# All of an expert's turned output tiles in one group after the second product, and the overflow scatter made dependent on the scatters before it

## The chip, the cores and the metric

The kernel runs on one core of a Trainium2 chip. TensorE (PE in the profile; PEld is its weight load) multiplies and transposes into PSUM, VectorE (DVE) and ScalarE (ACT) read PSUM and compute, GpSimd (POOL) issues the gathers and scatters, and SyncE (SP) issues the other transfers. The engines run side by side, each through its own list of instructions in order, and wait for each other on semaphores. The metric is the device time of one execution in microseconds (us); lower is better.

## The reference

A thresholded attention feeds a mixture of experts in which a hash of the token's id chooses the expert.

```python
# attention, per head: keep scores within tau of the row's maximum
scores = scale * np.matmul(q, k.transpose(0, 1, 3, 2))
thresh = np.max(scores, axis=-1, keepdims=True) - tau
scores = np.where(scores >= thresh, scores, -1e9)
attn = softmax(scores);  attn_out = np.matmul(attn, v)          # (8, 8, 576, 64)
x = attn_out.transpose(0, 2, 1, 3).reshape(4608, 512)
# experts: every token goes to one of 8
expert_idx = token_ids * np.int64(2654435761) % np.int64(8)
for e in range(8):
    mask = expert_idx == e
    out[mask] = np.maximum(x[mask] @ w1[e], 0) @ w2[e]          # 512 -> 1024 -> 512
```

With these inputs the experts get 598, 596, 571, 565, 599, 533, 570 and 576 tokens.

## The kernel before

The first 525 us are the attention, which the change does not touch. Then follow the experts, one after the other, some 59 us each. An expert has room for 600 tokens (CAP, as 19 blocks of 32 less 8). Tokens beyond the 600th would be taken by a loop at the end of the program (`For_i`, L1038), which runs once for each tile of 128 overflow tokens; its trip count is loaded from `ov_i` (L1037). No expert here has more than 599 tokens, so the loop's body is not entered; but the instructions that load the count, compare it, branch and wait stand in the program on every engine.

Layer 1 and layer 2 of an expert are each computed by `seven`: a matrix product done as seven block products with sums on DVE before and after. `layer1` calls it twice (g = 0 and 1), `layer2` once. A block product takes one PSUM tile from `bank2()`; the pool `ps_m` has four of these[...]. A fifth `bank2()` has to wait until an earlier tile has been read. In this text the products of one `seven` are numbered 1 to 7 in their order: 1 gives p1 (copied by ACT), 2 gives c11, 3 gives u2, 4 gives u3, 5 gives c21, 6 gives u4 and c22, 7 gives c12. All but the first are read by an addition on DVE (L794). A hook, `side(g, step)`, is called after the products: step 0 after product 2, step 1 after 3, step 2 after 4, step 3 after 5.

Layer 2 leaves its result feature-major in `oT`. `put_out` brings it into token order: for each tile of up to 128 tokens, eight TensorE transposes into a `bank2()` (L923; two tiles of tokens share a bank2), one ACT copy into `o_sb` (L934), and one indirect scatter of the rows to `out` from POOL's queue (L938, in `put_rows`). The five tiles of expert e-1 are put out during layer 1 of expert e, g = 0: tiles 0 and 1 at step 0, tiles 2 and 3 at step 1, tile 4 at step 2. So one group of transposes stands between products 2 and 3, one between 3 and 4, one between 4 and 5. The pool `m_o` has three `o_sb` buffers: the copy of tile 3 waits until the scatter of tile 0 has landed, and that of tile 4 until the scatter of tile 1 has.

For the last expert tile 0 is put out within layer 2, tiles 1 to 3 in `middle`, within `last_tile`, and `last_tile` computes the remaining 120 tokens with plain products (L908), copies them with ACT into `o_end` (L912) and scatters those rows. The scatters of `put_rows` are declared to have no dependence on each other (`declare_no_dep`), since every token has one slot; the scatter inside the overflow loop belongs to the same group.

The order of each engine's instructions is written out by hand (`manual_schedule`), while the framework places the waits, picks the PSUM tile that a `bank2()` gets, and splits the program into blocks around the loop. In the built program the scatter of `o_end` stands on POOL's list behind the loop, after a block in which each engine waits for every transfer and every other engine.

Of the kernel before, what the change touches and what calls it, by code (L numbers as in the profile page):

```python
# [9 lines left out]
FP32 = mybir.dt.float32  # L10
# [10 lines left out]
def kernel(  # L21
# [12 lines left out]
    nc = tc.nc  # L34

    B, H, D, S = qT.shape
    N, DIN = out.shape
    E, _, F = w1.shape
    P = 128
    HP = H // 2  # L40
    NP = B * HP
    CO = DIN // P
# [14 lines left out]
    KT, NB = 5, 19  # L57
# [4 lines left out]
    FIRST = [P * k for k in range(KT)]  # L62
    TROWS = [P] * (KT - 1) + [CAP - FIRST[-1]]
# [19 lines left out]
    ident = consts.tile([P, P], FP32, name="ident")  # L83
# [16 lines left out]
    gidx = consts.tile([P, E, KT], I32, name="gidx")  # L100
# [30 lines left out]
    with tc.tile_pool(name="a_q", bufs=1) as a_q, \  # L131
# [25 lines left out]
        oT = a_o.tile([P, 64 + S], FP32, name="oT")  # L157
        av = ps_av.tile([P, 2, 512], FP32, name="av")
        kts, rss, recs, scs, nss, stats, ws = {}, {}, {}, {}, {}, {}, {}
# [112 lines left out]
        def turn_w(n, j):  # L272
            tr = ps_tr.tile([P, 2, 512], FP32, name="tr")
            if n % NS == 0:
                cols = [(64 + P * c, P * c) for c in range(NC)]
            else:
                cols = [(P * c, P * c) for c in (range(4), range(4, 9))[j]]
            turn(tr, w_bufs[n % NW], cols)
            return tr
# [354 lines left out]
        with tc.manual_schedule():  # L634
            make_identity(nc, ident[:])

            tr = ps_tr.tile([P, 2, 512], FP32, name="tr")
# [18 lines left out]
            for n in range(LAST + NS + 1):  # L656
                p, s = divmod(n, NS)
# [22 lines left out]
                q = p - 1  # L680
# [10 lines left out]
                if n == LAST:  # L691
                    for k in (0, 2):
                        tr = ps_sc.tile([P, 2, 512], FP32, name="sc")
# [11 lines left out]
                if turned:  # L705
                    tr = turn_w(m, 0)
# [6 lines left out]
                if n == LAST:  # L713
                    tr = ps_sc.tile([P, 2, 512], FP32, name="sc")
# [12 lines left out]
                if s in (3, 4) and turned:  # L727
                    tr = turn_w(m, 1)
# [11 lines left out]
                if s in (0, 1) and turned:  # L740
                    tr = turn_w(m, 1)
# [12 lines left out]
            for h in range(4):  # L754
                rows, n = slice(32 * h, 32 * h + 32), (NB - h + 3) // 4
# [3 lines left out]
            for g in range(4):  # L759
                rows, n = slice(32 * g, 32 * g + 32), min(KT, NB - KT * g)  # L760
# [6 lines left out]
            tr = ps_tr.tile([P, 2, 512], FP32, name="tr")  # L767
            early_xT(tr, 0, KT, CO - 1, CO)

    with tc.tile_pool(name="m_x", bufs=1) as m_x, \  # L770
# [3 lines left out]
        F2, C2, FH, D2, NG = F // 2, CO // 2, FO // 2, DIN // 2, FO // 4  # L774
        xT_bufs = [xT_0, m_x.tile([P, CO, CAP], FP32, name="xT_1")]
        xq = m_x.tile([P, DIN // 32, 32 * KT], FP32, name="xq")
        oT = m_x.tile([P, CO, CAP], FP32, name="oT")
# [7 lines left out]
        CHL = 32 * (NB - 4) // 2  # L785

        def bank2():
            return ps_m[0].tile([P, 2, 512], FP32, name="bank2")
# [40 lines left out]
        def sums_w2(e):  # L829
            s1 = None  # L830
            if e == E - 1:
                spare = w_pool.tile([P, CO, F], FP32, name="w1_sb")
                s1 = w_tiles["s1"] = spare[:, :, 0:D2]
            return left(*w2_blocks(w_tiles[e, 2]), triple(w2_s, 0, FH), s1)
# [4 lines left out]
        def sums_h(e, c0, c1):  # L839
            return right(*h_blocks(c0, c1, half2(e)), triple(h_s, c0, c1, half2(e)))  # L840
# [71 lines left out]
                nc.scalar.copy(o_sb[0:rows, c0:c1], ps[0:rows, 0, 0:c1 - c0])  # L912
            put_rows(o_sb[0:rows], idx[0:rows])

        def put_out(e, kts):

            tr = bank2()
            for i, kt in enumerate(kts):
                rows = TROWS[kt] if e < E - 1 or kt < KT - 2 else 2 * CHL - FIRST[kt]
                for co in range(CO):  # L920
                    for r in range(2):
                        half, c0 = slice(64 * r, 64 * r + 64), D2 * i + 64 * co
                        nc.tensor.transpose(tr[0:rows, r, c0:c0 + 64],  # L923
                                            oT[half, co, FIRST[kt]:FIRST[kt] + rows],
                                            ident[half, half])
            for i, kt in enumerate(kts):
                rows = TROWS[kt] if e < E - 1 or kt < KT - 2 else 2 * CHL - FIRST[kt]
                o_sb = m_o.tile([P, DIN], FP32, name="o_sb")
                dst = o_sb[0:rows].rearrange("p (c r q) -> p r c q", c=CO, r=2)
                src = tr[0:rows, :, D2 * i:D2 * i + D2].rearrange("p r (c q) -> p r c q", c=CO)  # L930
                if e == E - 1 and kt % 2:
                    nc.vector.tensor_copy(dst, src)
                else:
                    nc.scalar.copy(dst, src)  # L934
                put_rows(o_sb[0:rows], gidx[0:rows, e, kt:kt + 1])

        def put_rows(o_sb, idx):
            inst = nc.gpsimd.indirect_dma_start(  # L938
                out=out[:, :], out_offset=bass.IndirectOffsetOnAxis(ap=idx, axis=0),
                in_=o_sb, in_offset=None, bounds_check=N - 1, oob_is_err=False)  # L940
            inst = getattr(inst, "ins", inst)
            tc.declare_no_dep(inst, group="rows", reason="every token has one slot: distinct rows")
            tc.add_to_no_dep_group("rows", inst)

# [34 lines left out]
        with tc.manual_schedule():  # L979
            for e in range(E):  # L980
                more = e + 1 < E
                turns = turn_x(e + 1) if more else []

                if e > 0:
                    w2_work, h_work = sums_w2(e), sums_h(e, 0, 2)

                    def side1(g, step):
                        if g == 0:
                            run(w2_work)
                            if step == 0:  # L990
                                put_out(e - 1, (0, 1))
                            elif step == 1:
                                put_out(e - 1, (2, 3))
                            elif step == 2:
                                put_out(e - 1, (4,))
                        else:
                            run(h_work)
                        if step > 2:
                            run(turns, 1 if g == 0 else 2)

                    layer1(e, side1)
                    run(sums_h(e, 2, FH), 4)
                if e + 2 < E:
                    load_w1(e + 2)
                x_work = (sums_w1(e + 1) + sums_x(e + 1)) if more else []

                def side2(step):
                    if step == 0:
                        run(turns, len(turns))
                        if e + 2 < E:  # L1010
                            fetch(e + 2)
                    else:
                        run(x_work, 2)
                    if not more and step == 4:
                        put_out(e, (0,))

                layer2(e, side2)
                run(x_work, len(x_work))
                if e + 2 < E:
                    load_w2(e + 2)  # L1020


            def middle():
                put_out(E - 1, (1, 2))
                put_out(E - 1, (3,))

            last_tile(middle)

# [9 lines left out]
        with tc.For_i(0, n_ov, 1) as it:  # L1038
            ex = nc.values_load(ov_i[0:1, bass.ds(it, 1)], engines=[mybir.EngineType.Pool],
                                min_val=0, max_val=E - 1)  # L1040
            w1_sb = w_pool.tile([P, CO, F], FP32, name="w1_sb")
            w2_sb = w_pool.tile([P, FO, DIN], FP32, name="w2_sb")
            nc.gpsimd.dma_start(
                out=w1_sb[:],
                in_=w1[bass.ds(ex, 1)].rearrange("o (c p) f -> p (o c) f", p=P))
            nc.gpsimd.dma_start(
                out=w2_sb[:],
                in_=w2[bass.ds(ex, 1)].rearrange("o (c p) d -> p (o c) d", p=P))
            idx = m_x.tile([P, 1], I32, name="idx_ov")
            idx_odd = m_x.tile([P, 1], I32, name="idx_odd")  # L1050
            for table, dst in zip(slot_dram, (idx, idx_odd)):
                nc.gpsimd.dma_start(out=dst[:], in_=table[bass.ds(it * P + E * SL, P), :])
            nc.vector.tensor_tensor(out=idx[:], in0=idx[:], in1=idx_odd[:], op=ALU.min)
            gather(x_dram, xg_bufs[0][:], idx[:, 0:1])
            tr = bank2()
            for co in range(CO):
                nc.tensor.transpose(tr[:, 0, co * P:co * P + P], xg_bufs[0][:, co * P:co * P + P],
                                    ident[:])
            nc.vector.tensor_copy(xT_0[:, :, 0:P], tr[:, 0].rearrange("p (c q) -> p c q", c=CO))
            relu_layer(w1_sb, xT_0)  # L1060
            o_ps = bank2()
            for fo in range(FO):
                nc.tensor.matmul(o_ps[:, 0], lhsT=h_0[:, fo, 0:P], rhs=w2_sb[:, fo],
                                 start=(fo == 0), stop=(fo == FO - 1))
            o_sb = m_o.tile([P, DIN], FP32, name="o_sb")
            nc.scalar.copy(o_sb[:], o_ps[:, 0])
            put_rows(o_sb[:], idx[:, 0:1])


# [32 lines left out]
```

## Time and profile before

| | |
|---|---|
| median of 3 runs | 950.64 us (949.88 to 950.99) |
| the profiled execution | 951.87 us, of which the profile's span is 950.2 us |
| PE busy over the span | 935.2 us (98%) |
| DVE, ACT, POOL busy | 733.9, 478.6, 306.2 us |
| output transposes, L923 | 312 recorded, in 23 groups |
| copies of turned tiles, L934 and L932 | 37 and 2 |
| scatters of rows, L938 | 39 from `o_sb`, 1 from `o_end` |
| TensorE clock granted, mean | 0.996 |

A row of a timeline gives the start in us from the span's start, the busy time, the engine, the line, the operation with "output <- input", and the count of merged instructions; in square brackets stands the idle time of the engine before it and what ended it. The times of matmuls are starts that were recorded and ends that are modelled, so distances between starts are used here.

### The profile page before, as it was taken

Reading aid. Unit: us, or ns where it says so; the run is one execution under the profiler, and the core shown is the slowest. Engines: PE = TensorE matmul, PEld = TensorE weight load, DVE = VectorE, ACT = ScalarE, POOL = GpSimd, SP = SyncE. Lnnn points to the kernel's source line nnn. Section 1 sums busy time; section 2 is a strip of 40 time slices with the busy share of each in tenths; the row PEclk is TensorE's granted clock in tenths of the full one; section 3 lists DMA queues with packets and bytes.
Section 4 is the critical chain, followed back from the end, with each engine's and each line's share of the span. In section 5 each row is a group of like instructions: output and inputs, shape, how many; then the busy total and the mean of one; then the engine's idle time right before and its main releaser. Section 6 shows DMA issues by size and latency. Waiting matters only on the chain. (4 is left out here: it accounts for less than half of the span.)

```text
span 950.2 us, 21041 instructions
## 1 busy us (share of the span) xinstructions
PE 935.2 (98%) x7779; PEld 645.2 (68%) x7779; DVE 733.9 (77%) x1638; ACT 478.6 (50%) x778; POOL 306.2 (32%) x413
## 2 busy tenths in 40 slices
PE   7999999999999999999999999999999999999996
PEld 4666666666666666666667777777777777777784
DVE  7999999999999999999456756756667566575541
ACT  6988888888898898888320211202112031120310
POOL 4233233237766733565043300403013030110202
PEclk9999999999999999999999999999999999999999
DMA  7355456445438857841017444344443445311101
GB/s 177 87 142 131 107 134 148 100 124 137 105 90 212 210 158 156 196 103 35 26 37 216 156 93 174 96 147 160 115 151 91 143 157 142 128 55 32 50 1 51
DMA packets 113510, 113.31 MB, mean 119 GB/s; under 512 B 31182, under 2 KB 88014, under 8 KB 113408
## 3 DMA queue, kind: packets, MB, share of 16 engines
q1 hardware_dynamic: 105168, 92.84, 36.9%
q0 software_dynamic: 7808, 18.91, 6.7%
q8 instruction: 63, 1.03, 0.5%
q14 instruction: 39, 0.32, 0.1%
q10 hardware_dynamic: 432, 0.21, 0.1%
HBM read 81.99 MB, written 21.72 MB: 109 GB/s over the span
## 5 line engine op out<-in xcount | busy, mean ns | idle before, releaser
L247 ACT ACTIVATE w<-ns,nmx 128x576 f32<-128x576 f32 x288 | 220.3, 776 | 32.8 <-DVE ns L233 32.5
L258 DVE SCALAR_TENSOR_TENSOR w<-ns,thr,w 128x576 f32<-128x576 f32 x288 | 225.9, 816 | 0.7 <-POOL thr L240 0.6
L233 DVE TENSOR_SCALAR_CACHE_REDUCE ns<-sc 128x576 f32<-128x576 f32 x288 | 205.3, 744 | 4.4 <-PE sc L222 3.5
L222 PE MATMUL sc<-k_sb,q 64*128 64x288 f32 (+1 forms) x1280 | 178.7, 423 | 1.1 <-DVE drop L650 0.6
L269 PEld LDWEIGHTS tr<-ident,w 64*128 64x128 f32 x2624 | 106.6, 139 | 88.4 <-ACT wT_b L290 26.4
L240 POOL TENSOR_SCALAR thr<-nmx,drop 128x2 f32<-128x2 f32 (+1 forms) x160 | 103.4, 646 | 184.0 <-DVE ns L233 173.3
L938 POOL DMA_INDIRECT out_dram<-o_sb,gidx x39 | 47.7, 1222 | 292.3 <-ACT o_sb L934 278.9
L269 PE MATMUL tr<-ident,w 64*128 64x64 f32 x2624 | 139.0, 230 | 2.6 <-ACT wT_a L290 2.0
L869 ACT COPY p<-bank 128x600 f32<-128x600 f32 (+1 forms) x22 | 14.4, 654 | 201.4 <-PE bank L859 200.6
L222 PEld LDWEIGHTS sc<-k_sb,q 64*128 64x128 f32 (+1 forms) x1280 | 92.5, 178 | 23.1 <-DVE ns L233 9.9
L300 PE MATMUL av<-wT_a,v 128*64 128x320 f32 (+1 forms) x704 | 100.7, 419 | 0.0
L859 PE MATMUL bank<-h,w_sb 128*128 128x300 f32 (+1 forms) x384 | 97.3, 410 | 0.9 <-DVE h L609 0.9
L866 ACT ACTIVATE h<-h 128x600 f32<-128x600 f32 x56 | 39.4, 703 | 114.6 <-DVE h L794 114.1
L290 ACT COPY wT_a<-tr 128x512 f32<-128x512 f32 (+1 forms) x128 | 81.7, 638 | 19.8 <-PE tr L269 19.5
L859 PE MATMUL bank<-xT,w_sb 128*128 128x300 f32 x336 | 89.4, 416 | 0.0
L859 PEld LDWEIGHTS bank<-h,w_sb 128*128 128x128 f32 x384 | 72.9, 190 | 22.9 <-DVE h L609 1.3
L290 ACT COPY wT_b<-tr 128x512 f32<-128x512 f32 (+1 forms) x128 | 81.2, 635 | 6.6 <-PE tr L269 4.3
L300 PE MATMUL av<-wT_b,v 128*64 128x256 f32 x640 | 83.2, 389 | 0.0
L859 PEld LDWEIGHTS bank<-xT,w_sb 128*128 128x128 f32 x336 | 63.9, 190 | 21.0
L859 PE MATMUL bank<-h_s,w_s 128*128 128x300 f32 (+1 forms) x256 | 64.3, 410 | 0.0
L300 PEld LDWEIGHTS av<-wT_a,v 128*64 128x64 f32 x704 | 43.9, 137 | 28.8 <-issue 0.3
L859 PE MATMUL bank<-x_s,w_s 128*128 128x300 f32 x224 | 61.5, 423 | 0.0
(147 smaller groups left out, 1110.3 us busy)
## 6 DMA issues: line engine op xcount, KB each, us to landing
w_sb<-in_moe_w_dram SPq DMA_DIRECT2D x16, 2048.0 KB
q<-in_q_dram SPq DMA_DIRECT2D x62, 288.0 KB
v<-in_v_dram SPq DMA_DIRECT2D x32, 256.0 KB
x_scratch<-xm SPq DMA_DIRECT2D x32, 256.0 KB
xT<-xq SPq DMA_DIRECT2D x84, 80.0 KB
k_sb<-in_k_dram SPq DMA_DIRECT2D x31, 144.0 KB
k_sb<-in_k_dram SPq DMA_DIRECT2D x32, 112.0 KB
x_scratch<-xg SPq DMA_DIRECT2D x9, 256.0 KB
```

What stands on the lines that cost most here:

```text
L222: nc.tensor.matmul(sc[out_rows, i, 0:S2], lhsT=q_sb[rows, h, q0:q1], rhs=k_sb[rows, h], start=True, stop=True)
L233: nc.vector.tensor_scalar(out=ns[:].rearrange("p (i s) -> p i s", i=2), in0=sc[:, :, 0:S2], scalar1=-1.0, scalar2=None, op0=ALU.mult, op1= ...
L240: nc.gpsimd.tensor_scalar(out=thr[:, 0:j + 1], in0=stats[n][0][:, 0:j + 1], scalar1=drop[:], scalar2=None, op0=ALU.add)
L247: nc.scalar.activation(w, nss[n, j][:], AF.Exp, bias=stats[n][0][:, j:j + 1], scale=-1.0)
L258: nc.vector.scalar_tensor_tensor(out=w, in0=nss.pop((n, j))[:], scalar=stats[n][1][:, j:j + 1], in1=w, op0=ALU.is_le, op1=ALU.mult, accum_ ...
L269: nc.tensor.transpose(dst[:, r, 64 * c:64 * c + 64], src[rows, c0:c0 + P], ident[rows, rows])
L290: nc.scalar.copy(dst, tr[:, :, 0:64 * n_c].rearrange("p r (c q) -> p r c q", c=n_c))
L300: nc.tensor.matmul(av[64 * j:64 * j + 64, g, c0:c1], lhsT=v_sb[:, c, 64 * j:64 * j + 64], rhs=wT[g][:, i, c0:c1], start=(c == 0), stop=stop)
L859: nc.tensor.matmul(ps[:, i, 0:width], lhsT=x[:, c, c0:c0 + P], rhs=y[:, c], start=c == 0, stop=c == n_k - 1)
L866: nc.scalar.activation(c, c, AF.Relu)
L869: nc.scalar.copy(p1, product(a11, b11))
L938: inst = nc.gpsimd.indirect_dma_start(out=out[:, :], out_offset=bass.IndirectOffsetOnAxis(ap=idx, axis=0), in_=o_sb, in_offset=None, bound ...
```

## The change

`put_out` takes several groups of tiles. It first takes a `bank2()` for each group, then issues the transposes of all groups, and then the copies and scatters. During layer 1 it is called once, at step 0, with the groups (0, 1), (2, 3) and (4,); the calls at steps 1 and 2 are gone. In `middle` one call with (1, 2) and (3,) takes the place of two. `put_rows` gets a flag `ordered`; the overflow loop passes True, and its scatter is then left out of the group of scatters without dependences.

```diff
-        def put_out(e, kts):
-
-            tr = bank2()
-            for i, kt in enumerate(kts):
-                rows = TROWS[kt] if e < E - 1 or kt < KT - 2 else 2 * CHL - FIRST[kt]
-                for co in range(CO):
-                    for r in range(2):
-                        half, c0 = slice(64 * r, 64 * r + 64), D2 * i + 64 * co
-                        nc.tensor.transpose(tr[0:rows, r, c0:c0 + 64],
-                                            oT[half, co, FIRST[kt]:FIRST[kt] + rows],
-                                            ident[half, half])
-            for i, kt in enumerate(kts):
-                rows = TROWS[kt] if e < E - 1 or kt < KT - 2 else 2 * CHL - FIRST[kt]
-                o_sb = m_o.tile([P, DIN], FP32, name="o_sb")
...
+        def put_out(e, *groups):
+
+            def rows_of(kt):
+                return TROWS[kt] if e < E - 1 or kt < KT - 2 else 2 * CHL - FIRST[kt]
+
+            trs = [bank2() for _ in groups]
+            for tr, kts in zip(trs, groups):
+                for i, kt in enumerate(kts):
+                    rows = rows_of(kt)
+                    for co in range(CO):
+                        for r in range(2):
+                            half, c0 = slice(64 * r, 64 * r + 64), D2 * i + 64 * co
+                            nc.tensor.transpose(tr[0:rows, r, c0:c0 + 64],
+                                                oT[half, co, FIRST[kt]:FIRST[kt] + rows],
+                                                ident[half, half])
+            for tr, kts in zip(trs, groups):
+                for i, kt in enumerate(kts):
+                    rows = rows_of(kt)
+                    o_sb = m_o.tile([P, DIN], FP32, name="o_sb")
+                    dst = o_sb[0:rows].rearrange("p (c r q) -> p r c q", c=CO, r=2)
+                    src = tr[0:rows, :, D2 * i:D2 * i + D2].rearrange("p r (c q) -> p r c q", c=CO)
+                    if e == E - 1 and kt % 2:
+                        nc.vector.tensor_copy(dst, src)
+                    else:
+                        nc.scalar.copy(dst, src)
+                    put_rows(o_sb[0:rows], gidx[0:rows, e, kt:kt + 1])
+
-        def put_rows(o_sb, idx):
+        def put_rows(o_sb, idx, ordered=False):
             inst = nc.gpsimd.indirect_dma_start(
                 out=out[:, :], out_offset=bass.IndirectOffsetOnAxis(ap=idx, axis=0),
                 in_=o_sb, in_offset=None, bounds_check=N - 1, oob_is_err=False)
             inst = getattr(inst, "ins", inst)
+            if ordered:
+                return
             tc.declare_no_dep(inst, group="rows", reason="every token has one slot: distinct rows")
             tc.add_to_no_dep_group("rows", inst)
...
                             if step == 0:
-                                put_out(e - 1, (0, 1))
-                            elif step == 1:
-                                put_out(e - 1, (2, 3))
-                            elif step == 2:
-                                put_out(e - 1, (4,))
+                                put_out(e - 1, (0, 1), (2, 3), (4,))
...
             def middle():
-                put_out(E - 1, (1, 2))
-                put_out(E - 1, (3,))
+                put_out(E - 1, (1, 2), (3,))
...
             nc.scalar.copy(o_sb[:], o_ps[:, 0])
-            put_rows(o_sb[:], idx[:, 0:1])
+            put_rows(o_sb[:], idx[:, 0:1], True)
```

In the built program the order changes in two places. On PE the 40 transposes of an expert stand together between products 2 and 3. On POOL the scatter of `o_end` stands ahead of the loop's instructions instead of behind them. The orders on ACT and DVE stay as they were.

More of the change, by code (lines that the diff above doesn't have):

```diff
@@ L913, in last_tile @@
             put_rows(o_sb[0:rows], idx[0:rows])
-        def put_out(e, kts):
-            tr = bank2()
-            for i, kt in enumerate(kts):
-                rows = TROWS[kt] if e < E - 1 or kt < KT - 2 else 2 * CHL - FIRST[kt]
-                for co in range(CO):
-                    for r in range(2):
-                        half, c0 = slice(64 * r, 64 * r + 64), D2 * i + 64 * co
-                        nc.tensor.transpose(tr[0:rows, r, c0:c0 + 64],
-                                            oT[half, co, FIRST[kt]:FIRST[kt] + rows],
-                                            ident[half, half])
-            for i, kt in enumerate(kts):
-                rows = TROWS[kt] if e < E - 1 or kt < KT - 2 else 2 * CHL - FIRST[kt]
-                o_sb = m_o.tile([P, DIN], FP32, name="o_sb")
[L929 to L935, printed above, removed]
```

## The prediction

> **What bounds the kernel now.** I read the page's first part, then the timeline of one expert boundary, the waits of the expert stage, and the end.
>
> ```profile
> PE 935.2 (98%) x7779; PEld 645.2 (68%) x7779; DVE 733.9 (77%) x1638; ACT 478.6 (50%) x778; POOL 306.2 (32%) x413
> ```
>
> TensorE never rests for long; in the expert stage a window of 24.40 us (761.9 to 786.3) has DVE busy 15.26, ACT 7.55 and POOL 9.32 us. What shortens TensorE's chain there shortens the kernel, unless a product then waits for its PSUM tile. The timeline at the fifth of the seven groups (layer 1 of e = 5), with the rows that the change touches:
>
> ```profile
> 766.13 0.72 PE L923 MATMUL bank<-ident,oT 64*128 64x64 f32 x16
> 766.30 0.78 DVE L794 TENSOR_TENSOR h<-bank,p 128x600 f32<-128x600 f32 x1 [3.33 <-PE bank L859]
> ...
> 766.77 2.29 PE L859 MATMUL bank<-x_s,w_s 128*128 128x300 f32 x8
> 767.00 1.22 DVE L791 TENSOR_TENSOR w_s<-w_sb 128x1024 f32<-128x1024 f32 x1
> ...
> 767.73 1.05 ACT L934 COPY o_sb<-bank 128x512 f32<-128x512 f32 x2
> 768.57 1.03 POOL L938 DMA_INDIRECT out_dram<-o_sb,gidx  x1 [34.03 <-ACT o_sb L934]
> ...
> 768.99 0.71 PE L923 MATMUL bank<-ident,oT 64*128 64x64 f32 x16
> ...
> 769.63 2.29 PE L859 MATMUL bank<-x_s,w_s 128*128 128x300 f32 x8
> ...
> 769.80 1.22 DVE L794 TENSOR_TENSOR w_sb<-w_sb 128x1024 f32<-128x1024 f32 x1
> 769.90 1.99 POOL L938 DMA_INDIRECT out_dram<-o_sb,gidx  x1 [0.30 <-issue]
> 771.43 0.58 ACT L934 COPY o_sb<-bank 128x512 f32<-128x512 f32 x1 [1.10 <-DMA out_dram<-o_sb,gidx]
> ...
> 771.85 0.43 PE L923 MATMUL bank<-ident,oT 64*88 64x64 f32 x8
> ...
> 772.21 2.29 PE L859 MATMUL bank<-x_s,w_sb 128*128 128x300 f32 x8
> ...
> 774.33 2.18 PE L859 MATMUL bank<-xT,w_sb 128*128 128x300 f32 x8
> ```
>
> Two things are to be seen. Products with transposes on both sides start 2.22 us before what follows them (766.77 to 768.99), the one with transposes ahead of it only 2.12 (772.21 to 774.33); the next starts 2.02 later, at 776.35. And ACT's fourth copy (771.43) did not wait for TensorE but for the landing of a scatter, because there are three `o_sb`. The end, from the timeline:
>
> ```profile
> 940.36 0.95 POOL L938 DMA_INDIRECT out_dram<-o_sb,gidx  x1 [0.30 <-issue]
> 941.55 0.27 ACT L912 COPY o_end<-bank 120x128 f32<-120x128 f32 x1 [1.27 <-PE bank L908]
> 944.94 1.02 POOL L938 DMA_INDIRECT out_dram<-o_end,gidx  x1 [3.63 <-issue]
> ```
>
> and, from the answer for the program's last line, the drains (shortest, median, longest in ns):
>
> ```profile
> L1098 POOLq DRAIN  x3: 46/109/4632, 944.7 to 949.9; - x3
> ```
>
> The last rows were ready at 941.82, but their scatter began at 944.94: it stands behind the loop's wait for all transfers, which ended with the landing of the scatter of 940.36, at 943.11. The closing drain on POOL took until 949.33.
>
> **The change part by part.** Time t is counted from an expert's first transpose (766.13 above).
>
> *Transposes on TensorE.* Before: 0.64 (16 transposes) + 2.22 + 0.64 + 2.22 + 0.36 (8) + 2.12, so product 6 starts at t = 8.20 (774.33). After: 40 transposes, then 2.12 + 2.02 + 2.02. Eight more transposes cost 0.64 - 0.36 = 0.28, so 40 cost 0.36 + 4 x 0.28 = 1.48; the 24 in one run in the last tile took 0.87 (936.06 to 936.93), which by the same steps gives 1.38. I take 1.42, and product 6 could start at t = 7.58: 0.62 less, 4.3 us for seven experts. If nothing waits.
>
> *The waits that come in their place.* Three groups now hold PSUM tiles at once, so the products behind them need these back sooner. The waits in the built program: product 3 waits for DVE's c11 (ends t = 0.95 by 766.30 + 0.78 less 766.13; needed at 1.42), product 4 for ACT's second copy (2.65; needed at 3.54). In the first group (e = 1) product 5 waits for u2, which DVE can finish at 1.42 + 2.32 + 0.78 = 4.5 (needed 5.56), and product 6 for the fourth copy. In the other six groups *product 5* waits for the fourth copy. That copy hangs on scatter 0, whose time the change leaves: c11's Relu, two copies, scatter at t = 2.45, landing 2.72 to 2.78 us later in five groups, 3.25 in the first and 3.24 in the last. The copy ended at t = 5.82 to 5.89 in five groups, 6.39 in the first, 6.34 in the last. Product 5 could start at 5.56. TensorE goes on 0.06 after an ACT copy (in the attention a copy ended at 300.35, the load began at 300.40). Five groups: product 5 at 5.90, product 6 at 5.90 + 2.12 = 8.02 instead of 8.20, saving 0.18 each. Last group: 6.40 + 2.12 = 8.52, losing 0.32. First group: its tile is asked for at 7.58, after 6.39, so the full 0.62. Sum: -0.62 - 5 x 0.18 + 0.32 = **-1.2 us**, of 4.3. Ends: -4.3 if no product waited, and +1.3 if all six landed at 3.25 (-0.62 + 6 x 0.32).
>
> Behind these waits: the tail products (6, 7 and g = 1) move with product 5. Product 7 needs the fifth copy, which ended at t = 8.2 at the latest and is wanted at 10.0. DVE's additions follow the products and have slack (15.26 of 24.40 us).
>
> *A rule that could spoil the fourth copy.* The Trainium skill (SBUF — State Buffer, "Who interferes with whom") says that a VectorE instruction with two SBUF inputs and a GpSimd instruction that reads SBUF exclude each other, and the one that started first holds the port to its end. The row shows it: scatter 1 (769.90) took 1.99 instead of 1.03, with DVE's `w_sb` sum (769.80 to 771.02) across its start. If such a sum fell across scatter 0, the fourth copy would come 1.0 later and six groups would lose 6 us. By the trace it doesn't: the `w_s` sum (t = 0.87 to 2.09) stays where it is, ahead of scatter 0 (2.45), and the `w_sb` sum moves later with u2, to about 4.4, after the start of scatter 1 (3.8). So I count nothing; scatter 1 may even get 1.0 shorter, which helps the fifth copy alone.
>
> *`middle`.* Its 24 transposes already stood together, orders and banks' readers stay: 0.
>
> *The scatter of `o_end`.* It no longer stands behind the loop's waits. It can start 0.28 after ACT's copy (768.57 less the first copy's end at 768.29), so at 942.10 instead of 944.94, and is issued by 943.12. POOL's own loading and testing of the count (about 1 us) now comes behind it, but beside its flight. It lands 2.7 to 3.3 later (2.70 and 2.74 for the two before it; 3.27 for itself): about 945.0. Then the block of waits: the slowest engine, DVE, left it 1.53 after the last landing before (943.11 to 944.63), so 946.5. POOL is at its drain by then. The drain is the unknown: it took 4.63 with the scatter ahead of it unfinished, 0.11 and 0.05 the other two times. Nothing is in flight now, so I take 0.1, the row it is like; the upper end is 4.63 again. From the drain's end to the span's end: 950.17 - 949.33 = 0.85. Sum: 946.5 + 0.05 + 0.85 = 947.4, **-2.75 us**. With a landing at 3.3: -2.4; with a second full drain (946.0 + 4.63 + 0.85 = 951.4): +1.3.
>
> *The ordered flag.* The loop's body isn't entered (the profile has no row of its lines), so its new waits cost 0; the flag's trace in this run is only the new place of the `o_end` scatter.
>
> Sum in the profiled execution: 951.87 - 1.2 - 2.75 = 947.9. The median of runs is 1.2 lower, 950.64, and both savings are distances that don't depend on that, so 950.64 - 3.95 = 946.7; a little of the landing spread taken in, **946.8 us**.
>
> **The rivals.** (a) Full gain: the fourth copy isn't waited for, because scatter 0 lands sooner or TensorE hides it; -4.3 - 2.7, 943.6. Against it, five groups agree on the landing within 0.06. (b) Late landings: scatters 0 and 1 now fly closer together (before, scatter 1 was held back by 1 us), and if all six groups show 3.25, the stage gives +1.3 and the sum is 949.2. Against: the scatters of 937.79 and 939.08 were also close, and landed in 2.68 and 2.70. (c) The end doesn't do what it should: the drain costs its 4.63 wherever it starts; +1.3 - 1.2, 950.7.
> (d) Slower: the clock. The Trainium skill (TensorE: Matmul & The Clock Gate, Part 4 and Part 1) says that transposes don't count as activity for the clock gate, and an idle window of 3.4 us halves the clock. By that rule a longer run of transposes could drop the clock in each of seven groups, each time for a window that does 1.7 us less work: +11.9 - 3.95, 958.6. The row of the window that holds the last group says otherwise (stretch, its length, busy us of PE, PEld, DVE, ACT, POOL, then the granted clock, DMA share, GB/s):
>
> ```profile
> 931.00:941.50 10.50, 10.50 (x69) 7.59 (x67) 1.94 (x3) 1.06 (x2) 3.92 (x4) 1.00 0.19 73
> ```
>
> It has the run of 24 transposes, and the clock is 1.00. 40 take 1.4 us, still well under such a window, with products around them. It decides only if the clock in the boundary falls below 1.00; a drop in two or three groups would eat the gain.
>
> **How the numbers follow.** My forecast, the end as worked out and part of the stage's gain, 945.6 to 948.7: 0.68. (a) 0.08; (b) and other small losses in the stage, 948.7 to 950: 0.12; (c) 0.07; (d) or a like stall 0.05. The range that leaves out (d), (c) and half of (a): 944.6 to 949.4. A measurement of this kernel can tell about 0.2%, 1.9 us, so faster means under 948.74: 0.68 + 0.08 + 0.03 = 0.79; slower, (d) and a little of (c): 0.06; same 0.15.
>
> **What would show it.** In the changed profile: one run of 40 transposes per expert, with the product behind it 1.4 us later; in six of seven groups a wait of TensorE for ACT's `o_sb` before product 5, some 0.3 us, 0.8 where the landing is late, and none in the first; a distance from first transpose to product 6 of 8.0 instead of 8.20; the scatter of `o_end` at about 0.3 after its copy; a closing drain of 0.1. I am wrong if the fourth copy moves, if the drain stays at 4.6, or if the granted clock falls.

## The result, and the profile after

The changed kernel took 948.48 us (median of 10 runs, 947.81 to 950.67) beside 951.04 us for the kernel before on the same chip (10 runs, 949.88 to 952.02). The ratio is 0.9976, with a 95% interval of 0.9967 to 0.9986: about 2.3 us less, between 1.3 and 3.1. The forecast was 946.8 us with a range of 944.6 to 949.4. The direction and the range held; the gain is smaller than the 3.8 us of the forecast (950.64, its median of before, less 946.8).

The profiled execution of the changed kernel took 950.67 us, the longest of its ten, with a span of 948.96 us; the one of before took 951.87, with 950.17. I split both spans at three marks that both traces have: the first output transpose (of e = 1), the last one (in the last tile), and the end of ACT's copy into `o_end`.

| stretch, us | before | after | difference | forecast |
|---|---|---|---|---|
| start to first output transpose (attention, first expert) | 530.93 | 531.70 | +0.77 | 0 |
| first to last output transpose ("the stage") | 405.86 | 404.38 | -1.48 | -1.2 |
| last transpose to the end of the `o_end` copy | 5.04 | 5.04 | 0 | 0 |
| end of the `o_end` copy to the end of the span ("the end") | 8.35 | 7.85 | -0.50 | -2.75 |
| span | 950.17 | 948.96 | -1.21 | -3.95 |

The first row is not the change's work: ahead of the first output transpose the program is the same, and in the other kernels below, with the same attention, this mark lies anywhere from 528.92 to 537.55 us. The two stretches that the change touches give -1.98 us together, inside the interval of the timed runs. So the stage did a little more than foretold, and the end did a fifth of it. Each stretch is read from one profile of each kernel; how well such readings repeat is told under "Each part alone".

Busy time hardly moved, as the page's first part shows (935.2 us of PE before):

```profile
PE 933.1 (98%) x7779; PEld 645.1 (68%) x7779; DVE 734.1 (77%) x1638; ACT 478.1 (50%) x778; POOL 306.1 (32%) x413
```

The timeline of the changed kernel at the fifth of the seven groups (start, busy us, engine, line, operation, count; in brackets the idle time before it and what ended it):

```profile
765.70 1.44 PE L927 MATMUL bank<-ident,oT 64*128 64x64 f32 x40
...
767.07 4.31 PE L859 MATMUL bank<-x_s,w_s 128*128 128x300 f32 x16
767.30 1.54 ACT L939 COPY o_sb<-bank 128x512 f32<-128x512 f32 x3
768.14 1.03 POOL L943 DMA_INDIRECT out_dram<-o_sb,gidx  x1 [34.03 <-ACT o_sb L939]
...
769.47 1.01 POOL L943 DMA_INDIRECT out_dram<-o_sb,gidx  x1 [0.30 <-issue]
770.09 1.21 DVE L794 TENSOR_TENSOR w_sb<-w_sb 128x1024 f32<-128x1024 f32 x1
...
771.00 0.58 ACT L939 COPY o_sb<-bank 128x512 f32<-128x512 f32 x1 [2.16 <-DMA out_dram<-o_sb,gidx]
...
771.64 2.29 PE L859 MATMUL bank<-x_s,w_sb 128*128 128x300 f32 x8 [0.26 <-ACT o_sb L939]
...
773.76 2.18 PE L859 MATMUL bank<-xT,w_sb 128*128 128x300 f32 x8
```

The 40 transposes stand in one run, and products 3 and 4 follow with nothing between them (one row, x16). The fourth copy waits for the landing of scatter 0, as it did before, and ends at 771.58; TensorE's product 5 starts at 771.64, after 0.26 us of idling for that copy. Product 6 starts 8.06 after the first transpose, 8.20 before. The view of waits, over the expert stage alone (525 to 950 us; us in total, times, longest), has two new rows for it:

```profile
PEld bank L859 <- ACT o_sb L939: 4.5, 6, 0.9
...
PE bank L859 <- ACT o_sb L939: 1.6, 6, 0.5
```

Six times, in six of the seven groups. The first group has no such wait.

The same view shows what the breaks themselves look like on the weight loads. In the kernel before:

```profile
PEld bank L923 <- issue: 6.9, 17, 0.6
PEld bank L923 <- ACT o_sb L934: 2.4, 6, 0.4
```

and in the changed one:

```profile
PEld bank L927 <- issue: 3.7, 9, 0.6
```

The six of the second row were no real wait for a copy. The copy that is named there, the second, had ended at t = 2.66 to 2.69 (t counted from an expert's first transpose, as in the prediction), 0.2 us before those transposes, and the weight loads stood idle for the same 0.405 us ahead of each of the 21 runs of transposes in the seven groups, whatever the view names. After the change there are seven such pauses in the groups, one for each.

At the end, the timeline and the drains of the program's last line (shortest, median, longest in ns, then the time of the first and the last):

```profile
940.85 0.27 ACT L912 COPY o_end<-bank 120x128 f32<-120x128 f32 x1 [1.27 <-PE bank L908]
941.41 1.02 POOL L943 DMA_INDIRECT out_dram<-o_end,gidx  x1 [0.81 <-ACT o_end L912]
```

```profile
L1100 POOLq DRAIN  x3: 46/103/2200, 945.9 to 948.7; - x3
```

The scatter of `o_end` starts 0.30 us after its copy instead of 3.12. But POOL's closing drain, which begins at 945.93 with everything landed (the last landing is at 944.83), still takes 2.20 us.

### The profile page after: what moved, and what is told of

It reads as the page before. It is cut to its first block, busy times and chain, and to the rows that moved or that the text cites. A ratio compares the mean times of both kernels' runs of the same rounds, so it can differ in the third digit from the quotient of the medians.

```text
span 949.0 us, 21042 instructions
## 1 busy us (share of the span) xinstructions
PE 933.1 (98%) x7779; PEld 645.1 (68%) x7779; DVE 734.1 (77%) x1638; ACT 478.1 (50%) x778; POOL 306.1 (32%) x413
## 3 DMA queue, kind: packets, MB, share of 16 engines
q8 instruction: 63, 1.03, 0.5%
## 4 chain that ended last, share of the span: by engine, by line
PE 58%; issue 31%; DVE 5%; POOL 2%; DMA 2%; ACT 1%; SPq 0%; POOLq 0%; DVEq 0%; ACTq 0%
PE av L300 16%; PE sc L222 14%; PE bank L859 13%; PE tr L269 10%; PE sc L587 3%; DVE w L258 2%; PE av L269 1%; DVE ns L233 1%; POOL out_dram L943 1%; DMA out_dram<-o_sb,gidx 1%; DVE xq L963 1%; ACT w L247 1%; POOL xg L113 1%; PE xT_ps L604 0%; PE sc L604 0%
## 5 line engine op out<-in xcount | busy, mean ns | idle before, releaser
L859 PE MATMUL bank<-x_s,w_s 128*128 128x300 f32 x224 | 59.6, 419 | 0.0
```

Of the source, the lines that this page charges most:

```text
L859: nc.tensor.matmul(ps[:, i, 0:width], lhsT=x[:, c, c0:c0 + P], rhs=y[:, c], start=c == 0, stop=c == n_k - 1)
```

## The experiments

All kernels are edits of the changed kernel ("after") or of the kernel before. Of the eight, the four kernels from "one group alone" to "before, five buffers" ran on one chip, where the kernel before had a median of 957.95 us (29 runs), the other four (two of them below under "The drain", one run each) on a second one, where it had 950.3 (19 runs). So absolute times are not compared across them; what I compare is the ratio to the kernel before on the same chip, and the two stretches of the table above in each trace, which don't hold the attention. Their results together:

| kernel | ratio and interval | that is, us | stage | end |
|---|---|---|---|---|
| before | 1 | 0 | 405.86 | 8.35 |
| after | 0.9976 [0.9967, 0.9986] | -2.3 | 404.38 | 7.85 |
| one group alone | 0.9988 [0.9972, 1.0003] | -1.1 | 404.55 | 8.41 |
| ordered scatter alone | 0.9990 [0.9973, 1.0007] | -1.0 | 405.85 | 7.93 |
| one group, five buffers | 0.9932 [0.9914, 0.9951] | -6.5 | 401.14 | 7.80 |
| before, five buffers | 0.9995 [0.9978, 1.0013] | -0.5 | 405.85 | 8.39 |
| two groups, five buffers | 0.9967 [0.9954, 0.9980] | -3.1 | 403.47 | 8.06 |
| one group, two buffers | 0.9951 [0.9938, 0.9964] | -4.7 | 401.80 | 8.45 |

"That is" is the ratio less one, times the median of before on that chip. A ratio's interval is some 1 to 2 us to either side, so the kernels are told apart by the stretches of their traces.

### Each part alone

After, without the ordered flag; the scatter of `o_end` falls back behind the loop:

```diff
-            put_rows(o_sb[:], idx[:, 0:1], True)
+            put_rows(o_sb[:], idx[:, 0:1])
```

> The grouping alone: the changed kernel without the ordered flag, so that the scatter of o_end stands behind the loop's waits again. Theory (the stage gives 1.5 us as the two profiles show, the end only about 0.5, since POOL's closing drain still takes 2.2): 1.5 us under the kernel before (0.9984), and the end of the profile as before: scatter of o_end 3.1 us after its copy, drain of some 4.6, 8.3 to 8.4 us from the last copy's end to the span's end. Rival (the end is worth its forecast 2.75 in an ordinary run, and the profiled run of the changed kernel, 2.2 above its median, had a slow end): the grouping alone is worth about nothing, 0.0 to 0.5 us.

Before, with the ordered flag and nothing else:

```diff
-        def put_rows(o_sb, idx):
+        def put_rows(o_sb, idx, ordered=False):
...
             inst = getattr(inst, "ins", inst)
+            if ordered:
+                return
...
-            put_rows(o_sb[:], idx[:, 0:1])
+            put_rows(o_sb[:], idx[:, 0:1], True)
```

> The ordered flag alone: the kernel before, with the overflow scatter made dependent, so that the scatter of o_end stands ahead of the loop. The transposes stay in three groups. Theory: 0.5 us under the kernel before, at most 1.0, with a closing drain of 2.0 to 2.4 and about 7.9 us from the last copy's end to the span's end. Rival: 2.7 us under it (0.9971), with a drain of about 0.1 and 5.6 us from copy to end.

Timed alone, each part is worth about 1 us, and both intervals reach over 1: the timed runs don't tell either part from no change. The traces do. With the group alone the stage is 404.55 (1.31 less than before) and the end 8.41, as before; with the flag alone the stage is 405.85, as before, and the end 7.93 (0.42 less). Each part acts in its own stretch only. The stage repeats well from profile to profile: 405.86, 405.85 and 405.85 in the three kernels with three runs of transposes, and 404.38, 404.55, 404.43 and 404.46 in the four with one run and three buffers. Their distances add up to -1.68 us (-1.31 + 0.06 - 0.01 - 0.42), 0.3 short of the -1.98 of both together; some 0.16 of that lies in the stage and 0.14 in the ends. The part in the stage is the last group: there the fourth copy of "one group alone" ended at t = 6.24 instead of 6.08, and product 6 started at 8.42 instead of 8.26.

The end of the first, from its timeline and its drains:

```profile
946.87 0.27 ACT L912 COPY o_end<-bank 120x128 f32<-120x128 f32 x1 [1.27 <-PE bank L908]
950.29 1.02 POOL L943 DMA_INDIRECT out_dram<-o_end,gidx  x1 [3.66 <-issue]
```

```profile
L1100 POOLq DRAIN  x3: 46/109/4657, 950.0 to 955.3; - x3
```

and of the second:

```profile
946.28 0.27 ACT L912 COPY o_end<-bank 120x128 f32<-120x128 f32 x1 [1.27 <-PE bank L908]
946.85 1.02 POOL L938 DMA_INDIRECT out_dram<-o_end,gidx  x1 [0.80 <-issue]
```

```profile
L1100 POOLq DRAIN  x3: 46/103/2200, 951.4 to 954.2; - x3
```

Late scatter: the drain's record begins at 950.04, before the scatter's at 950.29, takes 4.66 us, and runs beside the flight of that scatter, which lands at 953.6; it ends 1.12 after the landing. Early scatter: the flight is waited for first (landing 950.35, POOL at its drain 951.44), and then the drain takes 2.20, so that it ends 3.29 after the landing. The 2.8 us by which the scatter starts earlier are lost again to the drain, all but half a microsecond.

### Taking the copy's wait away

After, with five `o_sb` buffers, so that no copy has to wait for a scatter's landing:

```diff
-         tc.tile_pool(name="m_o", bufs=3) as m_o, \
+         tc.tile_pool(name="m_o", bufs=5) as m_o, \
```

> The changed kernel with five o_sb buffers instead of three, so that no copy of an expert's five tiles waits for a scatter of the same expert. Theory (product 5 waits for the fourth copy, and that for the landing of scatter 0): the wait is gone in all seven groups, product 6 starts 7.5 us after the first transpose in each, and the kernel gains a further 7 x 0.67 - 1.5 = 3.2 us over the changed one, some 5.5 us under the kernel before (0.994). Rival (the stage is held by something else, such as DVE's sums or the transposes themselves): same time as the changed kernel, and product 6 stays at 8.0 or is held by another wait.

The kernel before with the same edit, to see whether the buffers are worth something without the group:

> The kernel before with five o_sb buffers. Theory: its products don't wait for copies, so nothing moves, 0.0 within 0.3 us of the kernel before. Rival (the buffers alone are the gain of the run with group and five buffers): 2 us or more under the kernel before.

The timeline of "one group, five buffers" at the fifth group:

```profile
768.42 1.44 PE L927 MATMUL bank<-ident,oT 64*128 64x64 f32 x40
...
769.79 4.31 PE L859 MATMUL bank<-x_s,w_s 128*128 128x300 f32 x16
...
770.02 2.50 ACT L939 COPY o_sb<-bank 128x512 f32<-128x512 f32 x5
...
773.93 2.18 PE L859 MATMUL bank<-x_s,w_sb 128*128 128x300 f32 x8
...
775.95 2.18 PE L859 MATMUL bank<-xT,w_sb 128*128 128x300 f32 x8
```

The five copies run back to back, product 5 starts at t = 5.51 (773.93 less 768.42) and product 6 at 7.53, in all seven groups; the view of waits has no row any more in which TensorE waits for an `o_sb` copy. The stage is 401.14: 4.72 us less than before, or 0.67 for each of seven groups. On the kernel before, five buffers give nothing (405.85): its fourth copy comes a microsecond earlier, at t = 4.8, but product 6 stays at 8.21, since TensorE did not wait for that copy there. So the group's full worth is 4.7 us, and the wait for scatter 0's landing kept 3.2 of it from the changed kernel. This is the lowest ratio of the kernels tried, 0.9932, though its interval overlaps with that of two buffers below; the stretches give 5.3 us (4.72 and 0.55) where the ratio says 6.5, inside its interval.

### What one break of the products costs

If the gain comes from each return from products to transposes and back, merging only two of the three groups should give half. After, with five buffers and tile 4 put out later, at step 1:

```diff
                             if step == 0:
-                                put_out(e - 1, (0, 1), (2, 3), (4,))
+                                put_out(e - 1, (0, 1), (2, 3))
+                            elif step == 1:
+                                put_out(e - 1, (4,))
```

> Five o_sb buffers, and two groups of transposes for the three of before: tiles 0 to 3 behind the second product, tile 4 behind the third. If each group taken away saves the same (a fixed cost of going from products to transposes and back): half of the 4.7 us that all in one group saved in the stage from first to last transpose, so 403.5 us there (405.86 before, 401.14 with one group), and about 2.9 us under the kernel before. Rival (the gain comes from the transposes running longer in one go, or from the place behind the second product): 401 to 402 us.

Its timeline at the fifth group:

```profile
762.95 1.22 PE L927 MATMUL bank<-ident,oT 64*128 64x64 f32 x32
764.10 2.29 PE L859 MATMUL bank<-x_s,w_s 128*128 128x300 f32 x8
...
766.32 0.42 PE L927 MATMUL bank<-ident,oT 64*88 64x64 f32 x8
766.67 2.29 PE L859 MATMUL bank<-x_s,w_s 128*128 128x300 f32 x8
...
768.79 2.18 PE L859 MATMUL bank<-x_s,w_sb 128*128 128x300 f32 x8
770.81 2.18 PE L859 MATMUL bank<-xT,w_sb 128*128 128x300 f32 x8
```

Product 6 starts at t = 7.86 (770.81 less 762.95), between 8.20 and 7.53, and the stage is 403.47, half of the way from 405.86 to 401.14. Each break taken away is worth 0.33 to 0.34 us. The distances of the prediction and of the timeline of after say where it lies: the three runs of transposes of before took 0.64 + 0.64 + 0.36 = 1.64, the one run 1.37, so 0.27 for two breaks; and the three products took 2.22 + 2.22 + 2.12 = 6.56 until the next work started, and now 2.12 + 2.02 + 2.02 = 6.16, so 0.40. That is 0.67 for two. On the weight loads the pauses of 0.405 us follow the count of runs: 21 with three runs in each group, 14 here, 7 with one. What TensorE does in such a pause no run here shows.

### Making the copies later

The opposite of the five buffers: two, so that the third copy too has to wait for a landing. If late copies as such hold TensorE, this must be the slowest.

```diff
-         tc.tile_pool(name="m_o", bufs=3) as m_o, \
+         tc.tile_pool(name="m_o", bufs=2) as m_o, \
```

> The changed kernel with two o_sb buffers instead of three. The copies then wait longer: the third for the landing of scatter 0, the fourth for scatter 1 (to end at 7.2), the fifth for scatter 2. But the framework hands out the PSUM tiles in another order, and product 6 rather than 5 waits for the fourth copy. Theory (what counts is which product stands behind the late copy): no product waits, product 6 starts 7.5 us after the first transpose, the stage takes 401.2 us as with five buffers, and the kernel is 5 us or more under the kernel before. Rival (fewer buffers mean longer waits of TensorE): product 6 at 9.3, about 8 us slower than the changed kernel.

It was faster than three: 0.9951, with a stage of 401.80, where 401.2 was expected if no product waited at all. From its timeline at the fifth group:

```profile
761.42 1.44 PE L927 MATMUL bank<-ident,oT 64*128 64x64 f32 x40
...
766.75 0.59 ACT L939 COPY o_sb<-bank 128x512 f32<-128x512 f32 x1 [2.66 <-DMA out_dram<-o_sb,gidx]
766.94 2.18 PE L859 MATMUL bank<-x_s,w_sb 128*128 128x300 f32 x8
768.04 0.59 ACT L939 COPY o_sb<-bank 128x512 f32<-128x512 f32 x1 [0.71 <-DMA out_dram<-o_sb,gidx]
768.96 2.18 PE L859 MATMUL bank<-xT,w_sb 128*128 128x300 f32 x8
```

and from its waits over the expert stage:

```profile
PEld bank L859 <- ACT o_sb L939: 1.1, 2, 0.6
```

The copies are late: the third ends at t = 5.92, the fourth at 7.21, where with three buffers the fourth ended at 5.88. Yet product 5 starts at 5.52, before even the third copy has ended. So it can't stand in the PSUM tile of output tiles 2 and 3, as it does in six groups of the changed kernel. Product 6 does: in the one group where the fourth copy comes later still (the sixth, to t = 7.66), product 6 starts at 7.71 instead of 7.53, right behind it. That is how the first group of the changed kernel already stood, the only one there that did not wait. A product later, the same copy is no longer late. That the tile which a `bank2()` gets goes by the order in which tiles come free would explain the shift, but that is not shown; shown is only that the waiting product changes. Two of seven groups wait at all, 1.1 us together. The end got longer here (8.45), since the scatter of `o_end` started 0.99 after its copy, behind late scatters of `o_sb`.

### The drain

Two theories were left for the 2.20 us: the drain has a length of its own, or it waits for something that comes a fixed time after the last landing. To delay the drain past that, I put idle copies on ACT behind the last tile:

```diff
             last_tile(middle)
+            for _ in range(13):
+                nc.scalar.copy(halves[2][:], halves[1][:])
```

> What sets POOL's closing drain of 2.20 us, which the prediction took as 0.1. ACT copies one buffer into another 13 times after its last copy of o_end (work that nobody needs; ten of them stand ahead of the loop), so that the block of waits ends some 5 us after the last scatter has landed. Theory (the drain is work of a fixed length once the queue of scatters has been used): 2.2 us again, ending 7 us or more after the landing. Rival (the drain waits for something that ends 3.3 us after the last landing): it takes 0.1 to 0.2.

This one is inconclusive. In the built program only five of the thirteen copies stood ahead of the loop's block and eight behind it. The five ended before the last landing, so POOL came to its drain when it always does: landing 943.28, drain at 944.37 for 2.20 us. The eight behind (5.75 us) set the end of the program, 11.49 us after the `o_end` copy.

The other way to the same question is a program whose scatters ended long before. After, without any scatter of the last expert (the rows of that expert are not written):

```diff
-            put_rows(o_sb[0:rows], idx[0:rows])
...
-                    put_rows(o_sb[0:rows], gidx[0:rows, e, kt:kt + 1])
+                    if e < E - 1:
+                        put_rows(o_sb[0:rows], gidx[0:rows, e, kt:kt + 1])
```

> The changed kernel without the scatters of the last expert (its rows aren't written), so that the last transfer that POOL issued lies about 45 us before the end. Theory (fixed length): the drain takes 2.2 us again, and from the last copy of o_end to the span's end it is 2.2 + 2.2 = 4.0 to 5.0 us instead of 7.9. Rival (the drain depends on scatters near the end): 0.1 to 0.2, and 2 to 3 us to the end.

One run took 943.7 us, with a span of 941.99. The copy, and the drains:

```profile
938.39 0.27 ACT L912 COPY o_end<-bank 120x128 f32<-120x128 f32 x1 [1.27 <-PE bank L908]
```

```profile
L1100 POOLq DRAIN  x3: 46/103/1792, 939.4 to 941.7; - x3
```

The last landing of a row lies at 892.3. The drain begins 47 us later and takes 1.79 us all the same. So it isn't waiting for that landing: most of the 2.20 us comes without any scatter near it. Another rival lies in the DMA records: an instruction load (queue 14) runs during each of the drains of 2.20 us. It ends 0.59 to 1.03 us before the drain does in the six profiles, while the drain's length doesn't change, so the drain doesn't end by it. In this run two such loads (queues 8 and 14) end at 940.6, 0.54 before the drain; what they have to do with its 1.79 us was not tested. The end came in under its expected 4.0 to 5.0 us, at 3.34, because POOL reached the drain only 0.71 after the copy's end; 0.71 + 1.79 + 0.84 is the 3.34. What the drain does in its time, what the 0.4 us between 1.79 and 2.20 are, and how a drain of 4.63 to 4.66 splits into its own length and the flight beside it, stays open.

## Why the prediction was right, and which term was mis-sized

The stage was foretold for the right reason. The end was to give 2.75 of the 3.95 us and gave 0.50, because the term for POOL's closing drain was 0.1 us and the drain took 2.20. That the total still fell into the range of 944.6 to 949.4 is owed to that range's width, not to this part of the working.

*Transposes in one run.* The prediction put a group's worth at 0.62 us if nothing waits. The first group of the changed kernel shows 0.67 (product 6 at t = 7.53), and with five buffers all seven show it. The 0.05 are the run of 40 transposes, put at 1.42 and measured at 1.37 from its start to the product behind it; the estimate from the 24 transposes, 1.38, was the better one.

*The waits in their place.* Right, and for the reason given: product 5 waits in six groups for the fourth copy, and this for scatter 0's landing. Foretold was product 6 at 8.02 in five groups; measured 8.05, 8.02, 8.02, 8.06, 8.02. The last group was to lose 0.32, with a landing of 3.24; the landing took 2.97 and the group lost 0.05. The first group saved 0.67 instead of 0.62. With these two the sum of the seven groups is -1.49, and the stage shows -1.48. The other side of the account, 4.3 us for seven groups without a wait, was measured with five buffers at 4.72, the seven times 0.05 more that the first group shows.

*The port.* The rule of the Trainium skill (SBUF — State Buffer, "Who interferes with whom"), that a VectorE instruction with two SBUF inputs and a GpSimd one that reads SBUF exclude each other, was weighed, and no loss was counted. Foretold was that no DVE sum would fall across the start of scatter 0, and that scatter 1 would get some 1.0 shorter. Scatter 1 took 1.01 at the fifth group, 1.99 before. Scatter 0 kept its 1.03. Not foretold: scatters 2 and 3 now take 1.37 and 1.72 there, where before they took 0.98 and 1.24. Scatter 2 starts at 770.79, within the `w_sb` sum of the fence above (770.09 to 771.30), and scatter 3 within the next. By these rows the exclusion moved from one scatter to two others; no copy of this group waits for those.

*The clock.* For rival (d) spoke the rule of the Trainium skill (TensorE: Matmul & The Clock Gate, Part 4) that transposes don't count as activity. The windows around the fifth and the last group of the changed kernel (stretch, length, busy us of PE, PEld, DVE, ACT, POOL, granted clock, DMA share, GB/s):

```profile
765.70:774.50 8.80, 8.54 (x68) 6.44 (x68) 6.28 (x7) 3.31 (x6) 5.14 (x5) 1.00 0.24 91
882.90:892.00 9.10, 8.64 (x69) 6.46 (x69) 6.32 (x7) 3.32 (x6) 5.37 (x5) 1.00 0.22 85
```

Both hold a run of 40 transposes, and the clock is 1.00. So runs of 1.4 us with products around them did not lower it; longer ones were not run.

*The end.* This is where the forecast was too good: 0.50 of 2.75 us. Its steps, counted from the end of the `o_end` copy: scatter at 0.28, measured 0.30. Landing 2.9 after that start by the forecast's 945.0, measured 3.42; the prediction had 3.3 as its late end, so this too was mis-sized, by 0.5. DVE out of the block 1.53 after the landing, measured 1.63. From the drain's end to the span's end 0.85, measured 0.84. And the drain: "Nothing is in flight now, so I take 0.1, the row it is like". It took 2.20. That is the term that was mis-sized. Because POOL leaves the block before DVE (945.93 against 946.46), not all of it shows: the drain ends at 948.13, and without it the end would by the prediction's own sum have followed DVE at 946.5, so by this estimate it costs 1.6 us; the later landing and the step to DVE cost the other 0.6 to 0.7. The row that was taken as like it was the wrong one. The drains of 0.11 and 0.05 us come after another drain on the same engine, a fraction of a microsecond later; the first drain after POOL's work was nowhere in the trace without a scatter under way, so its length could not be read off, and a value near the lower bound was chosen. The upper end that was kept, 4.63, was about as far off on its own side. Rival (c), "the drain costs its 4.63 wherever it starts", was wrong in its number and near in its meaning: by that estimate over half of the end's gain went there.

*The rivals of the stage.* (a), the full gain, needs that the copy isn't waited for; the waits refute it for this kernel, and with five buffers it is what happens. (b), landings of 3.25 in all groups, didn't come: in the five groups product 5 started at 5.90 to 5.94, as their earlier landings made it. Rival (d) fell with the clock's rows.

The sum by parts, with what the trace of after showed: -1.48 and -0.50, -1.98 us; the timed runs say -2.3 (-1.3 to -3.1). The interval holds it.

## What to carry to other kernels

When work of one kind is gathered on an engine, ask which buffer is now wanted earlier: here the gathering was worth 4.7 us, and one wait for the landing that frees the first of three buffers held 3.2 of that; two more buffers, worth nothing to the kernel before, gave it back. A step that is moved off the end saves only down to what else lies under it: work that ran beside the moved step (here the drain beside the scatter's flight) stands alone after the move, and its own length has to be measured. A short instruction of the same name is no measure of it unless it stands in the same place.

## What the runs showed of the hardware that was not expected

- POOL's closing drain takes 2.20 us when all transfers have landed (in six profiles, to the last digit), 1.79 when no row was scattered for 47 us, and 4.63 to 4.66 when a scatter is issued as it begins (three profiles).
- Each break of TensorE's products by a run of transposes costs 0.33 to 0.34 us beyond the work itself, whether one or two of three are taken away; ahead of each run the weight loads pause for 0.405 us.
- Fewer buffers were faster than three: two gave a stage of 401.80, three 404.38, five 401.14. Which product stands behind a late copy counted for more than how late the copy is.
- In these traces a scatter was held by a DVE sum that covers its start, and not by one that starts later: with the `w_sb` sum across it scatter 1 took 1.99 us; with that sum 0.6 us behind its start, and still within its run (770.09, for a scatter of 769.47 to 770.48), it took 1.01.
